# Moving the q and k casts ahead of rows they do not depend on, in POOL's queue, in a fused attention and MLP kernel

## Chip, cores and metric

One Trainium2 chip, one core. The time is device microseconds of that core; a figure such as "336.5 us" is a median of several executions. The profile is one execution, about 1.7 us shorter than its time because it runs from the first to the last instruction. Engines: PE does matmuls and transposes, ACT exp, relu and PSUM copies, DVE vector work, POOL casts and row scaling, SP issues most DMAs.

## The reference

```python
# q, k, v: (8 batches, 8 heads, 576, 64)
scores = q @ k^T / 8 ; keep 0 <= i - j < 64 ; softmax ; x = attn @ v      # window attention
xn = (x - mean) / sqrt(var + 1e-6) * g                                    # per row of 512
out = x + relu(xn @ w1) @ w2                                              # w1 512x2048, w2 2048x512
```

## The kernel before

The program runs in periods. In period g, PE does the MLP of batch g in units: first-layer units, then second-layer units. After unit i the work of "slot i" is issued: attention of batch g+1, and casts and transposes of batch g+2 (in period 1, of batch 3). Every engine gets its work in the order of issue, so a slot number decides what stands ahead of what on an engine: POOL started the casts of slot 24 at 97.55 us, after the row of slot 23 (its last operation at 96.84), though their loads had landed by 72.4. The last 64 rows of the batches are "tails", handled in periods 3, 5 and 7. Period 1 multiplies its second layer by plain matmuls (`ch`, L375), later periods by a seven-product scheme (`pA`, `pB`, `pC`, L435).

```python
def cast_qk(b, half):                  # POOL: two casts, q and k, f32 -> f16
    for x in range(2):
        t = qk32.pop((b, x, half)); dst = p_in.tile(..., tag=f"qk16_{x}")
        nc.gpsimd.tensor_copy(out=dst..., in_=t...)                  # L126
def t_main(b, x, half, eng=None):      # PE: eight transposes (L216), then a copy to qkT
    ...
def s_mm(g, j): ...                    # PE: one score block (L263); ACT: exp (L266)
def s_mask(g, j): ...                  # DVE: mask (L273)
def b_step(g, kb): ...                 # PE: attention times v (L291), reads vA and vB
                                       # DVE: divide into xn (L297), row statistics mvg (L302)
def z_step(g, kb):                     # POOL: normalised row, after the statistics
    nc.gpsimd.tensor_scalar(out=ve, in0=var, ...)                    # L316
    nc.gpsimd.tensor_tensor(out=rs, in0=ve, in1=mhalf, op=ALU.pow)   # L317
    nc.gpsimd.tensor_scalar(out=nm, ...)                             # L318
    nc.gpsimd.tensor_scalar(out=z, in0=xv, ...)                      # L319
def zt_step(g, kb): ...                # PE: transposes of z (L328); ACT: copy to zT
def make_vB(b):                        # two DMAs issued by POOL, SBUF to SBUF (L163, L164)
    ...
# ---- schedule, period 1 (cut) ----
    for j in range(4):
        at((9, 13, 16, 19)[j], s_mm, 2, j)
        at((13, 17, 20, 23)[j], b_step, 2, j)
        at((13, 17, 20, 23)[j], z_step, 2, j)
        at((19, 23, 26, 30)[j], zt_step, 2, j)
    at(8, load_qk, 3, 0) ; at(9, load_qk, 3, 1) ; at(14, load_v, 3, 0, 4)
    at(19, alloc_qkT, 3) ; at(19, cast_qk, 3, 0)
    at(21, alloc_v, 3)   ; at(21, cast_v, 3, 0, 2)
    at(22, cast_v, 3, 2, 4) ; at(22, alloc_vB, 3) ; at(22, make_vB, 3)
    at(24, cast_qk, 3, 1)
    for i, (x, half) in zip((24, 25, 28, 31), ((0, 0), (1, 0), (0, 1), (1, 1))):
        at(i, t_main, 3, x, half, 0)
    at(25, load_qk, 4, 0) ; at(26, load_qk, 4, 1) ; at(28, load_v, 4, 0, 4)
# ---- periods 2 to 5 (cut): rows at slots 2, 7, 12, 17; n = g + 2 ----
    at(13, alloc_qkT, n) ; at(13, cast_qk, n, 0) ; at(16, cast_qk, n, 1)
    # transposes at 17, 19, 21, 25
```

The softmax here doesn't subtract the row's maximum and nothing guards it: scores larger than these inputs give would overflow.

Of the kernel before, what the change touches and what calls it, by code (L numbers as in the profile page):

```python
# [20 lines left out]
def kernel(  # L21
# [11 lines left out]
    B, H, S, D = q.shape  # L33
# [603 lines left out]
    for g in range(NGRP):  # L637
        units, s_sums = mlp_units(g, (8, 16)[g] if g < 2 else 0, g == 0, g > 1)
        slots = [[] for _ in range(len(units) + 1)]

        def at(i, f, *a):
            slots[min(i, len(slots) - 1)].append((f, a))

        b = g + 1
        if g == 0:
            at(0, b_step, 0, 3)
            at(1, zt_step, 0, 2)
            at(3, zt_step, 0, 3)
            at(4, newton, 0, 0, 4)
            at(11, t_main, 1, 0, 0, 1)  # L650
            at(12, t_main, 1, 1, 0, 1)
            at(13, vB_cur, 1, 0, 1)
            at(13, vB_prev, 1, 0, 1)
            at(13, vB_cur, 1, 1, 1)
            at(13, vB_prev, 1, 1, 1)
            at(16, s_mm, 1, 0, True)
            at(17, s_mm, 1, 1, True)
            at(18, b_step, 1, 0)
            at(21, b_step, 1, 1)
            at(22, zt_step, 1, 0)  # L660
            at(24, zt_step, 1, 1)
            at(26, t_main, 1, 0, 1, 0)
            at(27, t_main, 1, 1, 1, 1)
            at(28, vB_cur, 1, 2, 0)
            at(28, vB_prev, 1, 2, 1)
            at(29, vB_cur, 1, 3, 0)
            at(29, s_mm, 1, 2, True)
            at(30, s_mm, 1, 3, True)
            at(30, load_v, 2, 0, 4)
            at(31, b_step, 1, 2)  # L670
        if g == 1:
            at(0, cast_qk, 2, 0)
            at(0, cast_qk, 2, 1)
            at(1, b_step, 1, 3)
            at(2, zt_step, 1, 2)
            at(13, newton, 1, 0, 4)
            at(5, zt_step, 1, 3)
            at(4, alloc_v, 2)
            at(4, alloc_qkT, 2)
            at(4, init_vB, 2)  # L680
            at(5, cast_v, 2, 0, 4)
            at(4, t_main, 2, 0, 0)
            at(4, t_main, 2, 1, 0)
            at(6, t_main, 2, 0, 1)
            at(6, t_main, 2, 1, 1)
            for c in range(4):
                at(7, vB_cur, 2, c, 1)
                if c < 3:
                    at(7, vB_prev, 2, c, 1)
            for m, i in enumerate((3, 2, 4)):  # L690
                at(22 + 3 * m, w2_sums, i, 0, 4)
                at(23 + 3 * m, w2_sums, i, 4, 8)
            for j in range(4):
                at((9, 13, 16, 19)[j], s_mm, 2, j)
                at((10, 14, 17, 20)[j], s_mask, 2, j)
# [3 lines that stand above are left out]
            at(8, load_qk, 3, 0)  # L699
            at(9, load_qk, 3, 1)  # L700
            at(14, load_v, 3, 0, 4)
            at(19, alloc_qkT, 3)
            at(19, cast_qk, 3, 0)
            at(21, alloc_v, 3)
            at(21, cast_v, 3, 0, 2)
            at(22, cast_v, 3, 2, 4)
            at(22, alloc_vB, 3)
            at(22, make_vB, 3)
            at(24, cast_qk, 3, 1)
            for i, (x, half) in zip((24, 25, 28, 31), ((0, 0), (1, 0), (0, 1), (1, 1))):  # L710
                at(i, t_main, 3, x, half, 0)
            at(25, load_qk, 4, 0)
            at(26, load_qk, 4, 1)
            at(28, load_v, 4, 0, 4)
        if g == 2:
            at(3, w2_sums, 1, 0, 4)
            at(4, w2_sums, 1, 4, 8)
        if g > 1 and b < B:
            for j in range(4):
                e = 2 if g == 2 and j == 0 else 0  # L720
                if j or g == 2:
                    at((e, 2, 7, 12)[j], s_mm, b, j)
                    at((e + 1, 3, 8, 13)[j], s_mask, b, j)
                at((2 + 2 * e, 7, 12, 17)[j], b_step, b, j)
                at((2 + 2 * e, 7, 12, 17)[j], z_step, b, j)
                at((8 + e, 13, 18, 23)[j], zt_step, b, j)
        for n, i in enumerate(TAILS.get(g, ())):
            ts = (10, 11, 14, 20) if n else (1, 2, 5, 11)
            at(ts[0], s_mm, NGRP - 1, i)
            at(ts[1], s_mask, NGRP - 1, i)  # L730
            at(ts[2], b_step, NGRP - 1, i)
            at(ts[2], z_step, NGRP - 1, i)
            at(ts[3], zt_step, NGRP - 1, i)
        n = g + 2
        if g > 1 and n < B:
            at(13, alloc_qkT, n)
            at(13, cast_qk, n, 0)
            at(16, cast_qk, n, 1)
            at(20, alloc_v, n)
            at(20, cast_v, n, 0, 2)  # L740
            at(21, cast_v, n, 2, 4)
            at(21, alloc_vB, n)
            at(21, make_vB, n)
            for i, (x, half) in zip((17, 19, 21, 25), ((0, 0), (1, 0), (0, 1), (1, 1))):
                at(i, t_main, n, x, half, 0)
            at(27, s_mm, n, 0)
            at(28, s_mask, n, 0)
            if n + 1 < B:
                at(17, load_qk, n + 1, 0)
                at(18, load_qk, n + 1, 1)  # L750
                at(23, load_v, n + 1, 0, 4)
        if g > 1:
            for i in range(1, 5):
                at(7 + i, s_sums, 0, 4, i)
                at(13 + i // 3, s_sums, 4, 6, i)
                at((15, 15, 19, 21)[i - 1], s_sums, 6, 8, i)
        for n, i in enumerate(TAILS.get(g + 1, ())):
            if n == 0:
                at(5, load_tail, i)
                at(24, cast_tail, i)  # L760
                at(27, t_tail, i, 0)
                at(29, t_tail, i, 1)
            else:
                at(25, load_tail, i)
        if len(TAILS.get(g, ())) == 2:
            at(3, cast_tail, TAILS[g][1])
            at(7, t_tail, TAILS[g][1], 0)
            at(8, t_tail, TAILS[g][1], 1)
        for i, u in enumerate(units):
            if g > 1 and i == 20:  # L770
                tbank["shared"] = True
            u()
            for f, a in slots[i]:
                f(*a)
        for f, a in slots[len(units)]:
            f(*a)
# [28 lines left out]
```

## Time and profile before

The median was 336.5 us (336.3 to 338.04, 3 runs); the profiled execution spans 334.9 us. From the page, the line of busy times, and two rows of the 40-slice table (a digit is a tenth; PEclk is the clock that was granted to PE):

```profile
PE 312.9 (93%) x3229; PEld 206.0 (62%) x3229; DVE 204.6 (61%) x388; ACT 176.7 (53%) x292; POOL 163.5 (49%) x251
...
PE   6998999999938998999899989998999999999993
...
PEclk9999999999978999999999999999999999999998
```

PE bounds the kernel; there is one deep hole in its row, and beside it two slices with a lowered clock. The table of waits for PE alone (what waited, for what: total us, times, longest) names the cause of the hole:

```profile
PE tp L216 <- POOL qk L126: 8.9, 5, 5.2
PE warm L564 <- DVE mbias L557: 2.9, 1, 2.9
```

Five times the transposes of q and k waited for the casts. The timeline of period 1 shows the longest (start, duration, engine, line, operation; in brackets the idle time before and its releaser):

```profile
85.46 2.52 POOL L126 CAST qk<-qk 128x1024 f16<-128x1024 f32 x2
...
90.02 0.76 POOL L319 TENSOR_SCALAR z<-xn,rsz 128x512 f16<-128x512 f32 x1
...
90.80 2.48 POOL L145 CAST vA<-v 128x1024 f16<-128x1024 f32 x2
...
93.69 0.74 POOL L163 DMA_DIRECT2D vB<-vA  x1
94.44 0.54 POOL L164 DMA_DIRECT2D vB<-vA  x1
...
96.84 0.76 POOL L319 TENSOR_SCALAR z<-xn,rsz 128x512 f16<-128x512 f32 x1
97.55 2.02 POOL L126 CAST qk<-qk 128x1024 f16<-128x1024 f32 x2
...
98.64 1.03 PE L216 MATMUL tp<-ident,qk 128*128 128x128 f16 x8 [5.22 <-POOL qk L126]
```

The second cast pair needs its loads, issued 33 us before, and no row. It stands behind v casts, two DMA issues and the last normalised row. PE stands still from 93.42 to 98.64. The table by stretches (busy time and instructions of each engine, then the granted clock, DMA share, GB/s) shows what follows:

```profile
core 0: us, PE busy (x) PEld busy (x) DVE busy (x) ACT busy (x) POOL busy (x), PEclk, DMA share, GB/s
94.00:96.00 2.00, 0.00 (x0) 0.00 (x0) 1.68 (x3) 0.00 (x0) 1.83 (x4) 1.00 0.76 189
96.00:98.00 2.00, 0.00 (x0) 0.00 (x0) 0.00 (x0) 0.00 (x0) 1.79 (x4) 0.61 0.45 123
98.00:100.00 2.00, 1.36 (x10) 1.08 (x11) 0.00 (x0) 0.29 (x1) 1.57 (x2) 0.50 0.09 14
100.00:102.00 2.00, 2.00 (x6) 0.65 (x5) 0.00 (x0) 0.73 (x1) 0.00 (x0) 0.50 0.82 278
102.00:104.00 2.00, 2.00 (x11) 1.06 (x10) 0.00 (x0) 0.50 (x1) 0.00 (x0) 0.68 0.97 310
```

The clock falls to 0.50 three microseconds into the gap (at about 96.4 us, from the shares of the rows) and is still 0.50 after PE has resumed (rows 98 to 102). A busy PE at 0.50 (row 100 to 102: six matmuls of 128x512) is a hidden cost of the wait. In the later periods the wait is short; here period 3, from the timeline:

```profile
157.41 0.54 POOL L316 TENSOR_SCALAR rsz<-mvg 128x1 f32<-128x1 f32 x1 [1.93 <-DVE mvg L302]
...
159.52 0.87 POOL L319 TENSOR_SCALAR z<-xn,rsz 128x512 f16<-128x512 f32 x1
...
160.60 3.98 POOL L126 CAST qk<-qk 128x1024 f16<-128x1024 f32 x4
...
161.69 0.62 PE L216 MATMUL tp<-ident,qk 128*128 128x128 f16 x8 [0.90 <-POOL qk L126]
```

POOL idles 1.93 us for the third row's statistics, with casts waiting behind. Last, at the start of period 2 (PE's timeline) two score blocks stand back to back, and the second waits for the exp of the first:

```profile
107.33 0.41 PE L263 MATMUL sc<-qkT,qkT 64*128 64x64 f16 x16
108.57 0.19 PE L263 MATMUL sc<-qkT,qkT 64*128 64x64 f16 x1 [0.83 <-ACT pt L266]
109.06 0.39 PE L263 MATMUL sc<-qkT,qkT 64*128 64x64 f16 x15 [0.30 <-ACT pt L266]
```

### The profile page before, as it was taken

How to read it: one execution, taken by the hardware profiler on the slowest of the kernel's cores; microseconds unless marked ns; L12 is line 12 of the kernel's file. 1: busy time of each engine (PE TensorE's matmuls, PEld its weight loads, DVE VectorE, ACT ScalarE, POOL GpSimd, SP SyncE). 2: the span in 40 equal slices, each digit the busy share in tenths (PEclk: the TensorE clock that was granted, in tenths of full speed). 3: DMA queues.
4: the chain of work that ended last, by engine and by line, in shares of the span. 5: the costliest groups of instructions: out<-in, count | busy, mean ns of one | idle time of the engine just before them, and what ended most of it. 6: DMA issues, size and time to landing. Idle time of an engine off the chain costs nothing.

```text
span 334.9 us, 7810 instructions
## 1 busy us (share of the span) xinstructions
PE 312.9 (93%) x3229; PEld 206.0 (62%) x3229; DVE 204.6 (61%) x388; ACT 176.7 (53%) x292; POOL 163.5 (49%) x251
## 2 busy tenths in 40 slices
PE   6998999999938998999899989998999999999993
PEld 4566445786514458755784578457845874585582
DVE  1895773776941696468653965587548845652543
ACT  1586525585415674578337844784468137604600
POOL 7588656503980179536932696269524614210000
PEclk9999999999978999999999999999999999999998
DMA  8999999956359907930599359500282092003013
GB/s 194 286 382 267 333 292 332 256 190 114 90 166 259 200 4 235 197 129 2 173 221 259 68 181 218 162 2 0 59 235 51 0 202 83 2 2 126 0 34 94
DMA packets 85638, 51.08 MB, mean 153 GB/s; under 512 B 55681, under 2 KB 76673, under 8 KB 85602
## 3 DMA queue, kind: packets, MB, share of 16 engines
q1 hardware_dynamic: 84816, 48.11, 52.4%
q0 software_dynamic: 640, 2.33, 3.0%
q8 instruction: 25, 0.41, 0.5%
q10 hardware_dynamic: 146, 0.13, 0.1%
q14 instruction: 11, 0.09, 0.1%
HBM read 38.80 MB, written 9.44 MB: 144 GB/s over the span
## 4 chain that ended last, share of the span: by engine, by line
PE 70%; DMA 11%; POOL 8%; DVE 4%; SPq 4%; issue 1%; ACT 1%; POOLq 0%; DVEq 0%; ACTq 0%
PE hps L363 24%; PE pA L435 9%; PE pC L435 7%; PE pB L435 7%; PE ch L375 6%; PE hph L484 4%; DMA qk<-in_q_dram 4%; PE tp L216 4%; DMA w2s<-in_moe_w_ch_dram 4%; PE xps L291 3%; PE sc L263 2%; PE ztp L328 2%; DMA out_dram<-xn 2%; SPq L139 2%; POOL qk L126 2%; DMA w1s<-in_moe_w_ch_dram 2%
## 5 line engine op out<-in xcount | busy, mean ns | idle before, releaser
L363 PE MATMUL hps<-zT,w1g 128*128 128x512 f16 x480 | 112.2, 379 | 0.0
L367 ACT ACTIVATE hrT<-hps 128x512 f16<-128x512 f32 x120 | 71.9, 599 | 36.1 <-PE hps L363 32.5
L363 PEld LDWEIGHTS <-w1g 128*128 128x128 f16 x480 | 44.1, 98 | 46.7 <-issue 1.0
L316 POOL TENSOR_SCALAR rsz<-mvg 128x1 f32<-128x1 f32 x28 | 12.0, 427 | 89.3 <-DVE mvg L302 72.8
L207 ACT COPY qkT<-tp 128x1024 f16<-128x1024 f16 x26 | 26.2, 1012 | 43.1 <-PE tp L216 42.8
L266 ACT ACTIVATE pt<-sc 128x512 f16<-128x512 f32 x72 | 39.0, 595 | 15.1 <-PE sc L263 13.8
L435 PEld LDWEIGHTS <-sS 128*128 128x128 f16 x448 | 43.0, 98 | 4.7
L126 POOL CAST qk<-qk 128x1024 f16<-128x1024 f32 x32 | 33.3, 1063 | 9.5 <-DMA qk<-in_q_dram 5.0
L331 ACT COPY zT<-ztp 128x512 f16<-128x512 f16 x36 | 21.1, 585 | 28.9 <-PE ztp L328 28.5
L435 PEld LDWEIGHTS <-hrT 128*128 128x128 f16 x336 | 32.2, 98 | 5.0
L442 DVE TENSOR_TENSOR xn<-pA,xn 128x512 f32<-128x512 f32 x28 | 19.2, 686 | 24.8 <-PE pA L435 22.0
L216 PE MATMUL tp<-ident,qk 128*128 128x128 f16 x256 | 20.6, 228 | 8.9 <-POOL qk L126 8.9
L414 DVE TENSOR_TENSOR sS<-hrT 128x512 f16<-128x512 f16 (+1 forms) x42 | 21.5, 511 | 10.2 <-ACT hrT L367 10.2
L297 DVE TENSOR_TENSOR xn<-xps,rcp 128x512 f32<-128x512 f32 x36 | 24.9, 692 | 4.3 <-DMA out_dram<-xn 3.1
L435 PE MATMUL pA<-wT,sS 128*128 128x256 f16 x224 | 26.9, 273 | 0.0
L435 PE MATMUL pC<-w2s,sS 128*128 128x256 f16 x224 | 26.8, 273 | 0.0
L294 DVE RECIPROCAL rcp<-xps 128x8 f32<-128x8 f32 x36 | 7.4, 204 | 31.5 <-PE xps L291 31.3
L273 DVE TENSOR_TENSOR pt<-pt,mask 128x1024 f16<-128x1024 f16 x28 | 19.0, 683 | 12.1 <-ACT pt L266 12.0
L299 DVE BATCH_NORM_STATS2 stats<-xn 128x6 f32<-128x512 f32 x36 | 25.0, 695 | 1.2
L216 PEld LDWEIGHTS <-qk 128*128 128x128 f16 x256 | 17.5, 102 | 13.0 <-POOL qk L126 10.1
L375 PE MATMUL ch<-w2s,hrT 128*128 128x512 f16 x96 | 25.3, 401 | 0.0
L319 POOL TENSOR_SCALAR z<-xn,rsz 128x512 f16<-128x512 f32 x28 | 23.5, 839 | 2.9
(85 smaller groups left out, 445.5 us busy)
## 6 DMA issues: line engine op xcount, KB each, us to landing
out_dram<-xn SPq DMA_DIRECT2D x34, 256.0 KB, 3.5
qk<-in_q_dram SPq DMA_DIRECT2D x16, 512.0 KB, 5.3
qk<-in_k_dram SPq DMA_DIRECT2D x16, 512.0 KB, 6.1
v<-in_v_dram SPq DMA_DIRECT2D x32, 256.0 KB, 6.3
w2s<-in_moe_w_ch_dram SPq DMA_DIRECT2D x12, 512.0 KB, 5.6
w1s<-in_moe_w_ch_dram SPq DMA_DIRECT2D x4, 512.0 KB, 6.6
tk<-in_k_dram SPq DMA_DIRECT2D x8, 256.0 KB, 4.6
tv<-in_v_dram SPq DMA_DIRECT2D x8, 256.0 KB, 4.7
```

What stands on the lines that cost most here:

```text
L126: nc.gpsimd.tensor_copy(out=dst[:, :].rearrange("p (a j) e d -> p a e j d", j=j), in_=t[:, :].rearrange("p (a e j d) -> p a e j d", e=2, j ...
L207: nc.scalar.copy(out=out, in_=in_)
L216: nc.tensor.transpose(out=tp[:, i, :], in_=src[:, i], identity=ident16)
L266: nc.scalar.activation(out=pt[:, par], in_=sc[par], func=AF.Exp, bias=0.0, scale=scale)
L297: nc.vector.tensor_tensor(out=xn, in0=xps[:, :, 0:D], in1=rcp_b, op=ALU.mult)
L299: nc.vector.bn_stats(out=stats, in_=xv)
L319: nc.gpsimd.tensor_scalar(out=z, in0=xv, scalar1=rs, scalar2=nm, op0=ALU.mult, op1=ALU.add)
L363: nc.tensor.matmul(out=hps, lhsT=w1g[:, kc, 128 * hc:128 * (hc + 1)], rhs=zT[g][:, kc, :], start=(kc == 0), stop=(kc == NKC - 1),)
L367: nc.scalar.activation(out=hrT[:, hc, :], in_=hps, func=AF.Relu, bias=0.0, scale=1.0)
L375: nc.tensor.matmul(out=ch[kb], lhsT=hrT[:, hc, 128 * kb:128 * (kb + 1)], rhs=w2s[:, hc, :], start=(hc == 0), stop=(hc == NHC - 1),)
L414: nc.vector.tensor_tensor(out=o, in0=x, in1=y, op=op)
L435: nc.tensor.matmul(out=bank[which][:, p, :], lhsT=a[:, c, 128 * p:128 * p + 128], rhs=wv[:, c, :], start=(first and p == 0 and c == 0), st ...
```

## The change

The intent: let POOL cast q and k in its idle time, ahead of rows that wait for statistics. In period 1 both cast pairs move forward, the transposes move about three slots forward, and the first score block of batch 3 moves in from period 2. In later periods the first cast pair goes ahead of the third row.

```diff
-            at(19, alloc_qkT, 3)
-            at(19, cast_qk, 3, 0)
+            at(13, alloc_qkT, 3)
+            at(13, cast_qk, 3, 0)
+            at(17, cast_qk, 3, 1)
 ...
-            at(24, cast_qk, 3, 1)
-            for i, (x, half) in zip((24, 25, 28, 31), ((0, 0), (1, 0), (0, 1), (1, 1))):
+            at(31, s_mm, 3, 0)
+            at(31, s_mask, 3, 0)
+            for i, (x, half) in zip((21, 24, 25, 28), ((0, 0), (1, 0), (0, 1), (1, 1))):
 ...
+        if g > 1 and g + 2 < B:
+            at(11, alloc_qkT, g + 2)
+            at(11, cast_qk, g + 2, 0)
         if g > 1 and b < B:
             for j in range(4):
-                e = 2 if g == 2 and j == 0 else 0
-                if j or g == 2:
-                    at((e, 2, 7, 12)[j], s_mm, b, j)
-                    at((e + 1, 3, 8, 13)[j], s_mask, b, j)
-                at((2 + 2 * e, 7, 12, 17)[j], b_step, b, j)
-                at((2 + 2 * e, 7, 12, 17)[j], z_step, b, j)
-                at((8 + e, 13, 18, 23)[j], zt_step, b, j)
+                if j:
+                    at((2, 7, 12)[j - 1], s_mm, b, j)
+                    at((3, 8, 13)[j - 1], s_mask, b, j)
+                at((2, 7, 12, 17)[j], b_step, b, j)
+                at((2, 7, 12, 17)[j], z_step, b, j)
+                at((8, 13, 18, 23)[j], zt_step, b, j)
 ...
-            at(13, alloc_qkT, n)
-            at(13, cast_qk, n, 0)
             at(16, cast_qk, n, 1)
```

## The prediction

> **What bounds the kernel now.** TensorE. The page gives PE 93% of 334.9 us busy, DVE 61%, ACT 53%, POOL 49%; the chain of waits is PE for 70%. Time comes off only where PE stands still or runs slowly. The wait table restricted to PE names one large cause: the q/k transposes (L216) waiting for the POOL casts (L126), 8.9 us in 5 waits. The timeline places them: 5.2 us in period 1 (PE idle 93.4 to 98.64 us) and 0.9 to 1.0 us in each of periods 2 to 5 (around 126, 161, 194, 230 us).
>
> **Why PE waits.** The casts could run early: their loads for period 1 were issued at 62.6 to 64.8 us. But POOL takes its queue in order. In period 1 the cast pair for half 1 stands behind the last normalised row, itself behind the v casts and two vB copies, and starts at 97.55. In periods 2 to 5 the casts stand behind the third row, which waits for its statistics (POOL idle 1.7 to 1.9 us before it).
>
> **A second cost of the long wait.** The table by stretches shows a granted clock of 0.50 from about 97 to 103.5 us; 128x512 matmuls come 0.43 us apart there instead of 0.22. [...] PE works at half rate from 98.64 to about 103.6: about 2.5 us lost.
>
> **What the change does.** No work is added or removed: POOL is reordered, the period 1 transposes move three slots earlier, and the first score block of batch 3 (with exp and mask) moves from period 2 to the end of period 1.
>
> - Period 1: casts (1.0 us each) fall in POOL's 2.4 us gap at 80.5 and after the second row. The wait and the slow clock go (7.7 us). Next in line is the last normalised row: still behind the v casts and vB copies, it should finish near 97, while PE would reach its transpose near 96.2. I put 1 us back, and 0.5 us for the score block now done here: PE should start period 2's first layer near 99.0 instead of 104.6. Gain 5.6.
> - Period 2: two score blocks back to back at 107.3 take 2.05 us, 1.1 us of it waiting for the exp. One, 0.4 us, remains. Gain 1.6.
> - Periods 2 to 5: the cast waits, 3.7 us in all, go. The third row is delayed by at most 0.5 us, and its transpose has 1 us of slack. Gain 3.7.
>
> Sum 10.9 us, all on the critical path, as PE is dense elsewhere: 336.5 - 10.9 = 325.6. With a little met by a new wait (batch 3's first attention-times-v, two slots earlier, against the vB copies, which land in 3.0 to 7.1 us) I say 326.0, range 323.5 to 329.5. Faster by over 2%: 0.91; within 2%: 0.08; slower: 0.01.
>
> **What would show it.** L216 waiting for L126 near 0; granted clock 1.00 through 90 to 115 us; the PE wait for the exp near 107 us gone; periods 2 to 5 each shorter by 0.9 to 1.0 us. Wrong steps would show as PE waiting over 1.5 us for the last z row of period 1, or for vB or exp results.
>
> **What would make it wrong.** [...] DMA crowding between 90 and 101 us, where batch 4's loads now start earlier, beside the vB copies[...].

The marked cuts take out a statement on the clock and two points on what could go wrong, which no trace showed at the time. They take no term out of the sum: it stays 5.6 + 1.6 + 3.7 = 10.9 us. That the clock would stay up without the wait was my estimate, from the one gap in the trace of the kernel before.

## The result, and the profile after

The median fell to 324.83 us (324.31 to 324.91, 3 runs). The ratio was 0.9636, 95% interval 0.9590 to 0.9682. A ratio here is the mean time of one kernel's fast runs over that of the other's of the same rounds, so it is not quite the ratio of the medians. Two repeats on other occasions gave 0.9633 and 0.9651. All outputs are right. The profiled execution spans 322.6 us. The page's lines:

```profile
PE 309.6 (96%) x3229; PEld 204.6 (63%) x3229; DVE 204.3 (63%) x388; ACT 176.8 (55%) x292; POOL 164.6 (51%) x251
...
PE   7978999999989999999999999999999999999993
...
PEclk9999999999999999999999999999999999999998
```

The hole and the lowered clock are gone. PE's table of waits no longer has the casts; its two longest entries are now:

```profile
PE warm L564 <- DVE mbias L557: 2.3, 1, 2.3
PE ztp L328 <- POOL z L319: 1.4, 1, 1.4
```

Period 1 in the timeline: the casts sit between rows, both pairs are done by 87.05, and what PE meets next is the last normalised row, still behind the v casts and the copies:

```profile
80.52 2.03 POOL L126 CAST qk<-qk 128x1024 f16<-128x1024 f32 x2
...
85.03 2.02 POOL L126 CAST qk<-qk 128x1024 f16<-128x1024 f32 x2
...
96.44 0.77 POOL L319 TENSOR_SCALAR z<-xn,rsz 128x512 f16<-128x512 f32 x1
...
97.26 0.40 PE L328 MATMUL ztp<-ident,z 128*128 128x128 f16 x4 [1.40 <-POOL z L319]
```

The stretches, same columns as before, keep a clock of 1.00:

```profile
96.00:98.00 2.00, 0.74 (x7) 0.51 (x8) 0.00 (x0) 0.30 (x1) 1.03 (x2) 1.00 1.15 279
98.00:100.00 2.00, 2.00 (x25) 0.92 (x24) 0.75 (x1) 1.39 (x4) 0.00 (x0) 1.00 1.03 257
```

Period 3 in the timeline: the first cast pair runs ahead of the third row, and the transposes follow without an idle mark 3 us later:

```profile
146.75 2.02 POOL L126 CAST qk<-qk 128x1024 f16<-128x1024 f32 x2
148.86 0.50 POOL L316 TENSOR_SCALAR rsz<-mvg 128x1 f32<-128x1 f32 x1
...
151.78 0.62 PE L216 MATMUL tp<-ident,qk 128*128 128x128 f16 x8
```

And in PE's timeline the two score blocks are apart, one at the end of period 1, one in period 2, neither waiting:

```profile
98.45 0.41 PE L263 MATMUL sc<-qkT,qkT 64*128 64x64 f16 x16
...
101.91 0.41 PE L263 MATMUL sc<-qkT,qkT 64*128 64x64 f16 x16
```

Where the time came from is clearest by period. A period is counted here from the first matmul of its first layer to that of the next, read from PE's timeline. The experiments are in the same table; each row is one profiled execution, in us.

| | P1 | P2 | P3 | P4 | P5 | P6 to the end |
|---|---|---|---|---|---|---|
| before | 45.50 | 35.86 | 34.39 | 33.80 | 34.62 | 91.6 |
| after | 39.87 | 32.84 | 33.31 | 32.83 | 33.30 | 91.5 |
| e1_steady | 45.90 | 34.79 | 33.46 | 32.83 | 33.30 | 91.5 |
| e2_p1casts | 39.84 | 35.86 | 34.27 | 33.80 | 34.48 | 91.5 |
| e3_noscore | 39.42 | 34.88 | 33.56 | 32.83 | 33.30 | 91.6 |
| e4_fill | 43.33 | 35.86 | 35.84 | 34.27 | 35.74 | 91.6 |
| e5_transposes | 47.38 | 35.96 | 34.45 | 33.79 | 34.28 | 91.5 |
| e6_rowfirst | 38.85 | 39.39 | 33.31 | 32.83 | 33.30 | 91.5 |
| e7_lateloads | 39.86 | 32.85 | 33.30 | 32.83 | 33.31 | 91.6 |
| e8_combined | 38.84 | 32.95 | 35.56 | 32.83 | 33.31 | 91.6 |
| e9_steadyfill | 43.24 | 34.79 | 34.91 | 33.09 | 33.31 | 91.5 |
| e1_again | 45.61 | 34.78 | 33.78 | 32.83 | 33.30 | 91.5 |

(What comes before period 1, setup and period 0, takes 58.8 to 60.1 us in all of them, with no part of the change in it.)

### The profile page after: what moved, and what is told of

It reads as the page before. It is cut to its first block, busy times and chain, and to the rows that moved or that the text cites. A ratio compares the mean times of both kernels' runs of the same rounds, so it can differ in the third digit from the quotient of the medians.

```text
span 322.6 us, 7813 instructions
## 1 busy us (share of the span) xinstructions
PE 309.6 (96%) x3229; PEld 204.6 (63%) x3229; DVE 204.3 (63%) x388; ACT 176.8 (55%) x292; POOL 164.6 (51%) x251
## 4 chain that ended last, share of the span: by engine, by line
PE 85%; DVE 4%; SPq 3%; DMA 2%; POOL 2%; ACT 1%; issue 0%; ACTq 0%; POOLq 0%
PE hps L363 33%; PE pA L435 11%; PE pC L435 8%; PE pB L435 8%; PE hph L484 6%; PE ch L375 4%; PE xps L291 4%; PE tp L216 3%; PE sc L263 3%; DMA w1s<-in_moe_w_ch_dram 2%; PE ztp L328 2%; SPq L139 2%; POOL w1g L188 1%; PE ch L499 1%; DVE wT L532 1%; SPq L87 1%
## 5 line engine op out<-in xcount | busy, mean ns | idle before, releaser
L363 PEld LDWEIGHTS <-w1g 128*128 128x128 f16 x480 | 44.1, 98 | 47.0 <-issue 1.0
L316 POOL TENSOR_SCALAR rsz<-mvg 128x1 f32<-128x1 f32 x28 | 12.2, 437 | 76.5 <-DVE mvg L302 75.5
L297 DVE TENSOR_TENSOR xn<-xps,rcp 128x512 f32<-128x512 f32 x36 | 24.9, 692 | 3.3 <-DMA out_dram<-xn 2.2
L273 DVE TENSOR_TENSOR pt<-pt,mask 128x1024 f16<-128x1024 f16 x28 | 21.2, 762 | 8.6 <-ACT pt L266 8.5
L484 PE MATMUL hph<-zT,w1g 128*128 128x256 f16 x192 | 23.6, 273 | 2.5 <-ACT zT L331 1.1
L375 PE MATMUL ch<-w2s,hrT 128*128 128x512 f16 x96 | 23.7, 380 | 0.1
L484 PEld LDWEIGHTS <-w1g 128*128 128x128 f16 x192 | 18.0, 98 | 5.8 <-issue 2.2
```

The source lines that it names most:

```text
L297: nc.vector.tensor_tensor(out=xn, in0=xps[:, :, 0:D], in1=rcp_b, op=ALU.mult)
L363: nc.tensor.matmul(out=hps, lhsT=w1g[:, kc, 128 * hc:128 * (hc + 1)], rhs=zT[g][:, kc, :], start=(kc == 0), stop=(kc == NKC - 1),)
L375: nc.tensor.matmul(out=ch[kb], lhsT=hrT[:, hc, 128 * kb:128 * (kb + 1)], rhs=w2s[:, hc, :], start=(hc == 0), stop=(hc == NHC - 1),)
L484: nc.tensor.matmul(out=hps[:, e], lhsT=w1g[:, kc, 128 * hc:128 * (hc + 1)], rhs=zT[g][:, kc, 256 * half:256 * half + 256], start=(kc == 0) ...
```

## The experiments

Three calls of four kernels, each call on one chip with its own runs of the kernel before (medians 337.53, 337.2 and 337.34 us). The expectations call my explanation "theory Q": POOL's queue order delays the casts, and the terms add up.

### e1_steady: only the later periods

```diff
+        if g > 1 and g + 2 < B:
+            at(11, alloc_qkT, g + 2)
+            at(11, cast_qk, g + 2, 0)
 ...
-            at(13, alloc_qkT, n)
-            at(13, cast_qk, n, 0)
```

> Only the part in periods 2 and later: the first cast pair ahead of the third normalised row; period 1 and the score block as before. Theory Q (POOL's queue order delays the casts, and each term adds up by itself): the four cast waits of 0.9 to 1.0 us in periods 2 to 5 vanish, the 5.2 us wait and the half clock of period 1 stay; gain 3.7 to 4.2 us, so about 332.5 us (ratio 0.988). Rival S (the gain comes from period 1 only; the later waits would be taken up again by z rows or DVE): about 336 us (ratio over 0.996).

Measured: 332.87 us, ratio 0.9848 (0.9801 to 0.9894). In its profile the one cast wait left is that of period 1, 5.2 us. Periods 2 to 5 are shorter by 1.07, 0.93, 0.97 and 1.32 us, together 4.3 us. Rival S falls: nothing took these waits up again.

### e2_p1casts: only the casts of period 1

```diff
-            at(19, alloc_qkT, 3)
-            at(19, cast_qk, 3, 0)
+            at(13, alloc_qkT, 3)
+            at(13, cast_qk, 3, 0)
+            at(17, cast_qk, 3, 1)
 ...
-            at(24, cast_qk, 3, 1)
```

> Only the two cast pairs of period 1 moved forward in the POOL queue; the transposes keep their old slots 24, 25, 28, 31 on PE and the score block of batch 3 stays in period 2. Theory Q: the place on POOL is all that matters; the 5.2 us wait and the half clock go, a wait of 1.4 to 1.9 us for the last z row appears, period 2 starts its first layer near 98.8 us instead of 104.6; gain 5.5 to 6, about 330.8 us (ratio 0.983). Rival T (the gain of period 1 needs the transposes earlier on PE too): gain under 3 us, over 333.5 us.

Measured: 331.73 us, ratio 0.9818 (0.9776 to 0.9859). Period 1 takes 39.84 us, as in the full change (39.87); the clock stays at 1.00 and the wait for the last row is 1.44 us. From its waits of PE (the first line holds the four short waits of periods 2 to 5, which this run leaves as they were):

```profile
PE tp L216 <- POOL qk L126: 3.7, 4, 1.0
...
PE ztp L328 <- POOL z L319: 1.4, 1, 1.4
```

Period 2 keeps its 35.86 us. So POOL's order alone saves 5.66 us in period 1. That does not make the earlier transposes worthless, because the full change also does a score block in period 1. e3_noscore below differs from e2_p1casts in period 1 by the transposes alone, and there period 1 takes 39.42 us: they are worth 0.42 us, about what the score block costs (0.45). In e2_p1casts PE waits 0.31 us for a mask at 88.49; with a transpose group standing before that row, as in e3_noscore, this wait is gone. The start of period 2 came at 99.6, not 98.8, because what comes before period 1 happened to be 0.7 us longer.

### e5_transposes: only the transposes of period 1

```diff
-            for i, (x, half) in zip((24, 25, 28, 31), ((0, 0), (1, 0), (0, 1), (1, 1))):
+            for i, (x, half) in zip((21, 24, 25, 28), ((0, 0), (1, 0), (0, 1), (1, 1))):
```

> The kernel before with only the transposes of period 1 moved to the new slots 21, 24, 25, 28; the casts keep their late places on POOL. Theory Q: PE runs into the late casts earlier and has more work left behind them: a wait of 1 to 1.5 us for the first pair, one of 6 to 8 us ending at the same 98.6 us for the second, half clock after it; slower than before by 2 to 4 us, about 339 us (ratio 1.006 to 1.012). Rival T (transposes earlier on PE give the gain of period 1): 2 us or more faster than before.

Measured: 338.6 us, ratio 1.0052 (1.0024 to 1.0081), a little less slow than I expected. PE's timeline shows both waits:

```profile
86.69 0.62 PE L216 MATMUL tp<-ident,qk 128*128 128x128 f16 x8 [1.00 <-POOL qk L126]
...
97.98 1.03 PE L216 MATMUL tp<-ident,qk 128*128 128x128 f16 x8 [6.06 <-POOL qk L126]
```

Period 1 is 1.9 us longer. A consumer moved forward without its producer only waits longer (6.06 us against 5.22). Rival T, that the earlier transposes make the gain of period 1, falls on both sides: without the casts they lose 1.9 us, and beside the casts they are worth 0.4.

### e3_noscore: the change without the moved score block

```diff
-            at(31, s_mm, 3, 0)
-            at(31, s_mask, 3, 0)
 ...  (and the block with "e = 2 if g == 2 and j == 0 else 0" as in the kernel before)
```

> The changed kernel, with the first score block of batch 3 put back into period 2, beside the second one. Theory Q: the two blocks back to back make PE wait about 1.1 us for the exp again (two waits near 101 us, 0.8 and 0.3 us), so 1.1 to 1.5 us slower than the changed kernel, about 326.1 us (ratio to before 0.968 to 0.969). Rival U (the wait for the exp near 107 us was an aftermath of the stall in period 1 and the slow clock): no such wait, same as the changed kernel, 324.8 us (ratio 0.964 to 0.965).

Measured: 327.19 us, ratio 0.9685 (0.9644 to 0.9727), against 0.9633 to 0.9651 for the full change. It was run at another time. The two exp waits are back, 0.83 and 0.30 us; the longer one in PE's timeline:

```profile
103.53 0.19 PE L263 MATMUL sc<-qkT,qkT 64*128 64x64 f16 x1 [0.83 <-ACT pt L266]
```

Period 2 takes 34.88 us against 32.84, so 2.04 us more; period 1 takes 0.45 us less. The move is worth 1.6 us on balance. Rival U falls: the exp wait is no aftermath of the stall. The ratios alone, with overlapping intervals, would not settle it; the stages do.

### e4_fill: keeping PE busy through the wait

```diff
+    def fill(n):        # n matmuls of mbias x ident16 into a score tile that nobody reads
 ...
+            at(28, fill, 21)
             for i, (x, half) in zip((24, 25, 28, 31), ((0, 0), (1, 0), (0, 1), (1, 1))):
```

> The kernel before, with 21 idle matmuls of 128x512 (about 4.5 us) on PE just before the transpose that waits 5.2 us in period 1; nothing else moves, the cast still comes at 98.6 us. Theory Q: PE is kept busy, so the granted clock stays 1.00 between 90 and 110 us, the wait shrinks to about 0.7 us, and the 5 us of work after it run at full rate: 2.0 to 2.6 us faster than before, about 334.1 us (ratio 0.993). Rival V (the half clock there has no cost on the critical path, or does not come from the idle gap): same as before, 336.5 us (ratio 0.998 to 1.002).

Measured: 336.93 us, ratio 0.9964 (0.9919 to 1.0009): inconclusive for the whole kernel. In the profile the mechanism is plain. PE's timeline, then the stretches of the same kernel:

```profile
93.75 4.70 PE L572 MATMUL fill<-mbias,ident 128*128 128x512 f16 x21
99.12 0.62 PE L216 MATMUL tp<-ident,qk 128*128 128x128 f16 x8 [0.68 <-POOL qk L126]
```

```profile
98.00:100.00 2.00, 1.32 (x13) 0.66 (x11) 0.00 (x0) 0.22 (x1) 2.00 (x3) 1.00 0.00 0
100.00:102.00 2.00, 2.00 (x14) 1.04 (x13) 0.00 (x0) 1.06 (x2) 0.05 (x1) 1.00 0.67 216
```

The cast comes no earlier, yet period 1 is 2.17 us shorter: 14 matmuls and transposes (four of them short, of a row) where the kernel before had 6 matmuls in the stretch from 100 to 102. Doing useless work gained time, because the clock stayed up (1.00 in both rows, 0.50 from 98 to 102 in the kernel before). But periods 3 and 5 were 1.45 and 1.12 us longer than before. There a tail's attention-times-v came late on PE, by 1.50 and 1.39 us. Its weights are the masked scores, and the mask (L273) stands on DVE behind a row whose L297 waited up to 2.3 us for an output store before it could reuse the row buffer (all such DVE waits: 6.3 us here, 3.1 before). The weight load in period 3:

```profile
146.83 0.34 PEld L291 LDWEIGHTS <-pt 128*64 128x64 f16 x16 [1.99 <-DVE pt L273]
```

(The profile puts the matmul's own wait down to L316 on POOL, which follows the same row and ends within 0.05 us of the mask.) So I repeated it on another base.

### e9_steadyfill and e1_again: the fill once more

The edit of e4_fill on the kernel of e1_steady, beside that kernel again.

> The fill of 21 idle matmuls again, now on the kernel with the early casts of periods 2 and later (e1_steady), whose later periods showed no wait that could hide it. Theory Q: period 1 is 2.0 to 2.4 us shorter than in the kernel without the fill (as in e4_fill: 43.3 us against 45.5), the granted clock stays 1.00, and this time the whole kernel is 1.8 to 2.4 us faster than e1_again. Rival V (what the clock costs in period 1 is given back later): same time as e1_again within 0.7 us.

> The kernel of e1_steady once more, as the yardstick for e9_steadyfill in the same rounds: 332 to 333 us (ratio about 0.986), period 1 45.5 to 46 us long with the half clock.

Measured: e9_steadyfill 331.44 us, ratio 0.9831 (0.9803 to 0.9858); e1_again 332.26 us, ratio 0.9853 (0.9823 to 0.9884). Period 1 is 2.37 us shorter (43.24 against 45.61) with the clock at 1.00, as theory Q says, but the whole kernel only by 0.8 us in the medians, and the intervals overlap. In the profiled execution period 3 is 1.13 us longer, with the same wait of a tail behind an output store (1.53 us). Theory Q is right for the stage, where the half clock costs 2.2 to 2.4 us; for the whole kernel the 0.8 us lies next to rival V's 0.7 and far from the 1.8 to 2.4 of theory Q. The runs without a fill point the same way: of the 33 timed executions of the kernel before, the six with a mean clock of 0.990 or more have a median of 336.8 us, the others 337.4. I show the giving back in the profiled executions only; that it explains the rest of the timed runs is an inference.

### e7_lateloads: is it the earlier loads?

```diff
-            at(25, load_qk, 4, 0)
-            at(26, load_qk, 4, 1)
             at(28, load_v, 4, 0, 4)
+            at(31, load_qk, 4, 0)
+            at(31, load_qk, 4, 1)
```

> The changed kernel with the q and k loads of batch 4 issued at the end of period 1, behind the v loads. Theory Q (only the POOL order counts): same as the changed kernel within 0.3 us, 324.8 us (ratio 0.963 to 0.966); the vB copies and v loads, with less beside them, land sooner. Rival X (part of the gain is that the casts free the input buffers earlier, so the next loads start earlier): 1 us or more slower than the changed kernel.

> The changed kernel itself, in the same rounds as the variants of it. Both theories: 324.3 to 325.1 us, ratio 0.964 to 0.966; it is the yardstick for the sub-1% differences.

Measured: e7_lateloads 325.01 us, ratio 0.9636 (0.9616 to 0.9656); the change in the same rounds 324.96 us, ratio 0.9633 (0.9613 to 0.9653). Equal, so rival X falls: the earlier q and k loads bring nothing. The vB copies landed after 3.7 and 5.8 us here and after 6.3 and 7.0 us in the change of the same rounds (a_again), with the q and k loads beside them; for the v loads no landing is given here.

### e6_rowfirst: taking the last wait away

```diff
-            at(22, alloc_vB, 3)
-            at(22, make_vB, 3)
+            at(23, alloc_vB, 3)
+            at(23, make_vB, 3)
```

> The changed kernel with the two vB copies (and their memset) of period 1 moved behind the last normalised row on POOL. Theory Q: the row is done 1.8 us earlier, the 1.4 us wait of its transpose near 97 us vanishes, and the vB copies, 2.3 us later, still land before their first use: 1.2 to 1.5 us faster than the changed kernel, about 323.4 us (ratio 0.960). Rival W (the vB copies are then late for batch 3's first attention-times-v, about 1 us or more of new wait there): same as the changed kernel or slower, 324.8 to 326 us.

Measured: 328.24 us, ratio 0.9711 (0.9679 to 0.9742). I expected 323.4, so this miss went to rival W, and further than it said. The wait for the row fell to 0.38 us and period 1 to 38.85 us, but the vB copies, issued 3.2 us later into busy DMA queues (DMA share 1.12 to 1.31 in the stretches from 96 to 104), took 7.5 us to land (PE's timeline and the stretches):

```profile
104.11 0.23 PE L291 MATMUL xps<-vB,pt 128*64 128x65 f16 x1 [3.63 <-DMA vB<-vA]
```

```profile
102.00:104.00 2.00, 0.00 (x0) 0.00 (x0) 0.00 (x0) 0.00 (x0) 0.00 (x0) 0.85 1.31 172
104.00:106.00 2.00, 1.89 (x34) 1.28 (x35) 1.13 (x3) 0.67 (x2) 0.00 (x0) 0.50 0.84 221
```

The wait ends with the landing of the first copy, at 103.97 us. In the gap of 3.63 us the clock again fell to 0.50, and period 2 grew by 6.55 us. This profile is the slowest of the six executions (329.76 us, mean clock 0.985). The two that kept a mean clock of 0.998 and 0.999 took 325.60 and 326.69 us, still 0.6 and 1.7 us more than a_again's median.

### e8_combined: the row first, and room for the copies

To the edit of e6_rowfirst it adds all loads of batch 4 at slot 31 (v first), and batch 3's first attention-times-v at slot 4 (with the transposes of its row at slot 10).

> The changed kernel with three more moves: the last normalised row of period 1 ahead of the vB copies on POOL (as in e6_rowfirst), all loads of batch 4 issued at the end of period 1, and batch 3's first attention-times-v at slot 4 of period 2 as in the kernel before. Theory Q: both waits are then out of the way, the z wait near 97 us (1.4 us) falls to under 0.5 and no wait for the vB copies over 0.3 us appears: 0.8 to 1.3 us faster than the changed kernel, about 323.8 us (ratio about 0.960). Rival W (the copies cannot be late by 2.3 us whatever the loads do): a wait for vB of 1 us or more, and no gain.

> The changed kernel again, as the yardstick for e8_combined: 324.5 to 325.3 us, ratio 0.962 to 0.966.

One statement there is wrong: the kernel before had this step at slot 6 of period 2, not 4 (and the prediction's "two slots earlier" is four). Measured: e8_combined 326.7 us, ratio 0.9692 (0.9663 to 0.9722); the change in the same rounds 325.6 us, ratio 0.9651 (0.9622 to 0.9681). Another miss: slower by about 1 us. Both waits did go: 0.36 us for the row, none for vB, period 1 at 38.84 us. But period 3 is 2.25 us longer: a tail's attention-times-v came 2.19 us late on PE, in the way seen in e4_fill. The SP queue and DVE in e8_combined's timeline:

```profile
124.79 7.95 SPq L139 DMA_DIRECT2D v<-in_v_dram  x4
132.84 3.79 SPq L401 DMA_DIRECT2D out_dram<-xn  x4
```

```profile
137.95 0.69 DVE L297 TENSOR_TENSOR xn<-xps,rcp 128x512 f32<-128x512 f32 x1 [2.73 <-DMA out_dram<-xn]
```

and SP in the changed kernel's timeline, from a_third:

```profile
125.81 4.12 SPq L139 DMA_DIRECT2D v<-in_v_dram  x4
130.46 3.39 SPq L401 DMA_DIRECT2D out_dram<-xn  x4
```

The issue of the next v loads, which stand ahead of the output stores on SP, took 7.95 us instead of 4.12, the stores went out 2.4 us later although the period ended 1.0 us earlier (131.39 against 132.40), and DVE waited for them. That batch 4's late loads held up the issue of the next ones is an inference. e7_lateloads also had late q and k loads, but no such DVE wait over 1.1 us, so it is the v loads, the row and copies, or the sum; that stays open. Issuing the v loads of later periods behind the stores would be the next thing to try; it was not run. No version beat the change.

## Why the prediction was right

I predicted 326.0 us (323.5 to 329.5); 324.83 was measured. Term by term, from the period table:

| term | predicted | measured | from |
|---|---|---|---|
| period 1, with the added score block | 5.6 | 5.63 | before and after |
| score block out of period 2 | 1.6 | 2.04 | e3_noscore and after, period 2 |
| cast waits, periods 2 to 5 | 3.7 | 4.3 | e1_steady, periods 2 to 5 |
| rest (before period 1, period 6 on) | 0 | 0.3 | before and after |
| sum | 10.9 | 12.3 (spans), 11.7 (medians) | |

- The cause. POOL's order was right: e2_p1casts saves 5.66 us in period 1 without touching PE's order, e5_transposes does the reverse and is slower, e7_lateloads rules out the earlier q and k loads. POOL held a cast pair whose loads had landed by 72.4 us until 97.55 us, behind the last row; issued ahead of it, the pair ran at 85.03.
- The second cost of the gap. I put 2.5 us on the half clock; e4_fill and e9_steadyfill measured 2.17 and 2.37 us in the stage. The clock was low from about 96.4 to 103.3 us (from the shares of the stretches), but PE works only from 98.64 on, so 4.6 us count, and half of that is 2.3 (eight 128x512 matmuls of L375 took 3.62 us from 99.47 on, twelve took 2.76 us from 84.52 on, at a clock of 1.00). This holds for the stage; in the medians of whole runs the fill gained 0.6 and 0.8 us, not clear of the noise.
- The new wait. I wrote that the last row would finish near 97 and PE reach its transpose near 96.2. It finished at 97.21; PE waited 1.40 us where I had put 1. This was the term most easily forgotten: the 7.7 us freed in period 1 became 5.6. That 5.6 was met to 0.03 us is partly luck. The pieces that the prediction lists give 7.7 - 1 - 0.5 = 6.2; its 5.6 comes from the two start times (104.6 and 99.0), and the difference is not explained there. The measured pieces are 5.22 for the wait and about 2.3 for the clock, less 1.40 for the new wait and 0.45 for the score block: 5.7.
- The score block. Period 2 gave 0.4 us more than I put. The two blocks take 2.06 us up to the next first-layer matmul in e3_noscore, one takes 0.34 in the change; the other 0.3 us was not traced.
- Periods 2 to 5. In period 2 POOL idled 1.24 us before the third row, not 1.7 to 1.9 as the prediction has it for all four. Each cast wait was worth slightly more than its mark in the wait table (3.7 us there, 4.3 in the periods). In period 5 the surplus is 0.4 us; the kernel before had there a 0.28 us wait of a tail, of the kind seen in e4_fill, and the change's profile shows none of that size. The rest I did not trace.
- The vB copies. I held back 0.4 us for them. They took 7.2 and 8.2 us from issue to landing (issued at 93.29 and 94.04 us), and the first use at 101.53 us shows no wait. It reads block 0 of vB, which only the first copy writes, landed at 100.46; the second, landed at 102.19, serves later rows. So the slack was 1.1 us: e6_rowfirst, which issues the copies 3.2 us later, waited 3.63.
- The terms add. By ratio, e1_steady saves about 5.1 us, e2_p1casts 6.1 and the score block some 1 to 2 us (each ratio times the 337 us of before); the change saves 12.

## What to carry to other kernels

Where an engine works through its queue in order, as POOL did here (a ready cast pair held until 97.55 us), put operations that are ready early ahead of those that wait for another engine, and count for each queue what stands in front of the operation that PE needs. A PE gap can cost more than its length: after each of the gaps of 3.63 us and more here PE resumed at half clock (0.50), after none of 2.19 us or less (1.00); lengths between were not tested. Price both, then look for the next event in line before booking the gain. When a kernel is this dense, a gain of 1 us in one stage is easily given back by DMA order in the next (e6_rowfirst: 1.02 us gained in period 1, 6.55 lost in period 2; e8_combined: 1.03 gained in period 1, 2.25 lost in period 3, with the cause partly inferred), so compare period by period, not only in total.

## What else the traces show of the hardware

- The granted clock. It fell to 0.50 in idle gaps of 5.22 (before), 6.06 (e5_transposes) and 3.63 us (e6_rowfirst) and not in gaps of 1.40 (after) and 2.19 (e8_combined). In the kernel before and in e6_rowfirst it stayed at 0.50 for 6.8 us (from the stretches); the return to 1.00 came 4.6 us (before) and 6.1 us (e6_rowfirst) after PE resumed. No run here was made to test what sets the time of the return.
- DMAs issued by POOL and by SP. The vB copies of batch 3, issued by POOL, took 3.1 to 5.8 us to land in before, e7_lateloads and e8_combined, with fewer SP loads beside them, and 5.9 to 8.2 in the three profiles of the change (in before SP issued no load from 90.7 to 98.6 us; in after it issued q and k loads at 90.45 and 91.00 and v loads from 94.55 on). Issuing takes time too: four v loads held the SP queue for 4.1 to 8.1 us, 1.0 to 2.0 each against a median of 6.3 from issue to landing in the kernel before, and the stores stood behind them (in e8_combined the v loads held the queue until 132.74 us, and the first store was issued at 132.84).
- POOL casts. A pair of 128x1024 f32 to f16 casts took 2.02 us, and 2.52 us in the kernel before at 85.46. The whole difference is in its second cast (1.55 us against 1.04), beside which DVE ran a tensor_tensor (L532) from 87.00 on. DVE was busy beside the pair of 2.02 us at 85.03 in the change too, so being busy alone is not it. That DVE caused it was not tested.
